# Joined small products, a split last tile and a new hand-written start in an attention-into-MLP kernel

## The chip, the core and the metric

The kernel runs on one core of one Trainium2 chip. The metric is the device time of one execution in microseconds (us), the median of several runs. The core has a matrix engine (TensorE, PE in the rows), VectorE (DVE), ScalarE (ACT), GpSimd (POOL) and a sync engine (SP) that issues most transfers. Each takes its own instructions strictly in order and waits at semaphores for the others. Matmul results go to PSUM banks of 128 rows by 512 fp32 columns; DVE and ACT carry them to SBUF.

## What is computed

```python
q_s = exp(q - max(q, -1)); q_s /= sum(q_s, -1) + 1e-9      # q, k, v: 8 x 8 x 576 x 64
k_s = exp(k - max(k, 2));  k_s /= sum(k_s, 2) + 1e-9       # k: softmax over the sequence
kv  = einsum('bhsd,bhde->...', k_s, v)                     # 64 x 64 per batch and head
x   = (q_s @ kv).transpose(0, 2, 1, 3).reshape(4608, 512)
h   = x @ w_in                                             # 512 x 2048
out = (h - tanh(h)) @ w_out                                # 2048 x 512
```

All is fp32. For the two large products, x, g = h − tanh(h) and both weights are split into a high and a low part, and three products (high·high, low·high, high·low) are added in PSUM.

## The kernel before

**Chunks and steps.** The 4608 tokens are worked on in 9 chunks of 512: one per batch, and one that collects the last 64 tokens of every batch. A chunk has 16 steps, one for each 128 columns of w_in. In a step TensorE makes `ph` (12 matmuls of 512 columns, `h_mm`), then ACT and DVE turn it into g by the chain u, t, vv, mk (ACT) and g, t, g, g (DVE); ACT casts the high part `gh`, and POOL or DVE subtracts it to get the low part `gl`. Two steps later (`LAG`) TensorE adds g times w_out into four banks `po`, one for 128 tokens each (`o_mm`, 12 matmuls). There are 144 steps. After a chunk's last step `o_out` copies the four `po` banks to SBUF and `o_store` writes them out.

**Small products.** Each batch also needs k^T v (`pk`, `kv_mm`) and q·kv (`px`, `x_mm2`). Both are fp32 matmuls: a `pk` has three parts, pk0 (first half of v, 16 instructions), then pk1 (second half, 16, and the last 64 rows, 8); a `px` has two halves px0 and px1 of 16 instructions each. They are spread over the steps of the chunk before. A bank from the pool `ps_m` holds each. The `px` halves are then cast to `xh` (ACT) and subtracted to `xl` (DVE), which the next chunk's `ph` reads. `v_ones` fills the tile of v for pk1 with columns of ones by POOL before its transfer.

**Order.** Up to step 33 the string `ORDER` names every operation one by one, in program order; a `*` picks the other engine (for `gl`, `sub`, `qu` and `qn` POOL without a star and DVE with one, for `cl` the reverse, for `ca` and `qs` ACT without). `phN` and `poN.t` are the large products of step N, `pk0@2` is batch 2's first `pk` part, `ld`, `cl`, `lo`, `pr`, `st`, `ca` and `sub` are the load and the splitting of one weight tile (`sub`, L213, makes its low part), `warm` are fp32 matmuls whose result nobody uses (`warm5h` is five; the trace counts an fp32 matmul as two), `out@b` and `in@b` send the maxima of k to memory and bring them back in a row shape (`rows<-most`, `row<-rows`), and `ks` subtracts them. From step 19 on the table `PLACES`, with `MOVED` for single batches, names for each of these the slot of a step (`first`, `ph`, `mid`, `sums`, `end`, `act`, `dve`, `dve2`, `pool`, `post`, `sp`) and the step counted from the chunk's start.

Of the kernel before, what the change touches and what calls it, by code (L numbers as in the profile page):

```python
# [37 lines left out]
sq3 px0 sub.i2 ld.i6 pr.i1 mq2 px2 xh0.1 xh0.0 ld.o5 warm10h st.i1 qu2 xh2.1 xl0.0 ca.i1 warm4h
sa3 ld.o3 xl0.1 xh2.0 lo.i3 sr3 xl2.0 qn6 qe2 xl2.1 ph0 ld.o2 km1.a vo1.2 lo.i5 sub.i1 sq2 lo.o0
v1.1 ca.i4 cl.i5 ph1 cl.o0 pr.i5 sa2 cl.i3 t0 km1.b ld.i7 u0 sr2 km1.c pr.i3 qn4 tt0 vv0 ph2 g0  # L40
pr.o0 st.i3 u1 t1 gg0 m0 km1.d vv1 cl.o1 pm1 ca.i3 st.o0 pt6 lo.o1 mx1 sub.i3 ph3 ca.o0 cp0 u2
mh1 g1 sub.i4 gh0 tt1 lo.i6 ml1 gg1 vo1.0 m1 qn7 v1.0 pb1 pr.o1 v1.2 cp1 ph4 t2 st.i5 cl.o2* m2
ld.o4 ks1.2 ld.i13 gh1 ld.o6 sub.o0* ca.i5 gl0 ld.o7 vv2 ks1.0 ld.o12 t3 u3 sub.i5 ph5 ks1.1
ld.i10 pr.o2 lo.o3 g2 gl1 ke1.0 qs6* ld.o8 pt4 gg2 ke1.1 qn5 po0.3 ld.i11 tt2 u4 po0.1 g3 qs4
cl.i6* po0.2 ld.o15 tt3 ke1.2 pt5 lo.o2 st.o1 cl.i7* pk1.0 cp2 qs5 ld.o9 vv3 st.o2 pk1.1 ca.o1
gg3 ld.i12 m3 sub.o1 pr.i6 cp3 pk1.2 t5 ld.o11 po0.0 st.i6 ca.o2 cl.o5 po1.1 lo.i7 cl.o3 cl.o4
gh2 po1.3 sub.o2* m4 gl2 po1.2 sl1 tt5 t4 pt7 pr.o3 rs1 rc1 po1.0 ca.i6* lo.o4 st.o3 po2.0 pr.o5
sub.i6 tt4 pr.i7 po2.1 g4 vv4 po2.2 st.i7 gh3 po2.3 u5 gg4 gl3 ph6 ca.i7 kn1 cp4 vv5 keep@1
pr.o4 sub.i7 g5 qs7* m5 st.o4 ca.o3 px4 lo.o5 cl.i12 gg5 ph7 lo.o6 sub.o3* ca.o4 ld.i9 cp5 xh4.1
ld.o10 sub.o4 u6 ld.o13 xl4.1 gh4 ld.o14 st.o5 k@2.2 xh4.0 po3.0 cl.o9 u7 po3.2 gl4* ld.i15  # L50
ca.o5 xl4.0 px6 t6 sub.o5 lo.o7 tt6 po3.3 cl.i10 xh6.0 ld.i14 cl.o6* po4.0 m6 xl6.0 po3.1 pr.i10
g6 cl.o15* po4.2 gh5 cl.o7* po4.3 xh6.1 gl5* vv6 po4.1 v@2.2 v@2.0 cl.i11* lo.i10 v@2.1 po5.0 g7
ld.i8 pr.o6 po5.1 gg6 cl.i9* xl6.1 po5.3 vv7 st.o6 ph8 t7 pr.i12 tt7 ca.o6 cp6 lo.i11 gg7 m7
cl.i15 pr.o7 po5.2 sub.o6* gh6 ph9 cl.o11 t8 st.o7 gl6 u8 cp7 vv8 tt8 lo.i12 g8 gh7 po6.0 st.i12
pr.i9 po6.2 gg8 m8 po6.1 ca.o7* lo.i8 gl7* po6.3 t9 sub.o7 lo.i15 ph10 tt9 cp8 u9 st.i10 gh8 g9
# [18 lines left out]
po20.0 exp0@2.0 gg22 ph25 cp22 u23 gl21* vv23 kf@2.0 t23 most@2.0 po20.1 po20.2 g23 out@2.0
po21.2 gh22 tt23 po21.1 t25 gl22* u25 po21.0 gg23 mu23 po21.3 cp23 in@2.0 po22.2 keep@0 sum0@2.0
gh23 po22.0 ph24 gl23* n01@2.0 tt25 g25 po23.0 n00@2.0 ks0@2.1 u24 po22.3 t24 po22.1 vv24 g24
mu24 ph26 gg24 tt24 vv25 gg25 cp24 po23.1 ks0@2.0 gh24 po23.2 t26 ph27 f01@2.0 mu25 ke0@2.0
gl24* cp25 out23.0 tt26 out23.1 u26 po23.3 g26 po24.1 gh25 ks1@2.0 pk0@2.0 vv26 t27 gg26 out23.2
ph28 gl25* mu26 v1@2.0 u27 f00@2.0 vv27 tt27 q1@2.0 g27 out23.3 po25.1 u28 cp26 po24.3 ke1@2.0
gg27 po24.2 mu27 po24.0 store23.2 vv28 v1@2.1 ph29 t28 v@2.3 ker@2.0 store23.1 gh26 gl26* cp27  # L80
po25.2 u29 g28 po25.0 max1@2.0 po25.3 po26.3 gh27 po26.2 mu28 gg28 sub1@2.0 t29 po26.0 tt28 vv29
po26.1 cp28 pk1@2.0 gl27* gh28 pk1@2.1 ph30 den@2.0 v@3.2 g29 v@3.0 den@2.1 den@2.2 tt29 gg29
gl28* po27.2 u30 den@2.3 po27.1 den@2.4 mu29 keep@2.0 po27.0 exp1@2.0 cp29 po28.2 g30 mu30
po27.3 sum1@2.0 vv30 k@3.0 po28.3 t30 k@3.2 gh29 px0@2.0 k@3.1 gl29 v@3.3 ph31 xh0@2.0 n11@2.0
xl0@2.0 gg30 n10@2.0 xh0@2.1 f11@2.0 po28.0 tt30 t31 back po28.1 f10@2.0 u31 cp30 po29.1 q0@3.0
# [954 lines left out]
```

## Time and profile before

| | |
|---|---|
| time, median of 3 runs | 882.75 us (882.49 to 883.05) |
| profiled execution | 882.5 us, its span 880.7 us |
| granted TensorE clock, mean | 0.998 |
| TensorE busy | 854.2 us, 97% of the span |
| VectorE busy | 668.8 us, 76% |
| ScalarE, GpSimd busy | 523.1 us (59%), 271.2 us (31%) |
| first matmul, last matmul's end | 14.40 us, 876.71 us |

The span runs from the first to the last instruction of the core; 1.8 us of the execution lie outside it. A row of a timeline gives the start, the duration, the engine, the line, the operation with its tiles, and in brackets the idle time ahead of it with the engine that ended it. Names are those of the program without their numbers.

### The profile page before, as it was taken

What the parts mean: (1) busy time and instruction counts of PE and PEld (TensorE: products, weight loads), DVE (VectorE), ACT (ScalarE), POOL (GpSimd) and SP (SyncE); (2) the same over time, 40 slices, a digit from 0 to 9 for tenths busy, and PEclk for the clock granted to TensorE, in tenths of its full rate; (3) what the DMA queues carried; (4) which work ended last, traced back from release to release, by engine and by line L of the source; (5) the groups of instructions that cost most, each with busy time, mean ns of one, the idle gap of its engine ahead of it and who ended that gap; (6) DMA issues with size and microseconds to landing.
All of it is one profiled execution on the core that took longest, in us unless ns stands there. A gap on an engine that the chain in (4) does not pass through costs nothing.

```text
span 880.7 us, 13278 instructions
## 1 busy us (share of the span) xinstructions
PE 854.2 (97%) x4860; PEld 699.7 (79%) x4860; DVE 668.8 (76%) x1102; ACT 523.1 (59%) x914; POOL 271.2 (31%) x233
## 2 busy tenths in 40 slices
PE   3999999989999999999999999999999999999998
PEld 2877888768788888888888888888888888888886
DVE  7898999978887879678867787768866776655444
ACT  4887987546455556555665565555555555555553
POOL 3664222111233323332234233323323333322221
PEclk9999999999999999999999999999999999999999
DMA  9996130004523315331432232322261011002001
GB/s 258 329 316 208 45 76 1 0 19 109 131 85 49 90 25 60 49 91 24 60 49 61 54 52 50 68 55 19 43 96 32 1 48 25 1 1 49 1 0 48
DMA packets 127873, 61.17 MB, mean 69 GB/s; under 512 B 72768, under 2 KB 118848, under 8 KB 127808
## 3 DMA queue, kind: packets, MB, share of 16 engines
q1 hardware_dynamic: 127808, 60.32, 30.5%
q8 instruction: 38, 0.62, 0.3%
q14 instruction: 27, 0.22, 0.1%
HBM read 48.76 MB, written 11.55 MB: 68 GB/s over the span
## 4 chain that ended last, share of the span: by engine, by line
PE 82%; DVE 10%; DMA 3%; ACT 2%; issue 2%; SPq 0%; DVEq 0%; ACTq 0%
PE po L853 39%; PE ph L775 38%; DVE g L809 2%; PE pk L364 2%; DMA rows<-most 2%; PE px L631 2%; DVE g L804 1%; DVE g L796 1%; PE warm L233 1%; DMA row<-rows 1%; DMA k<-in_k_dram 1%; DVE t L801 1%; DVE k L350 1%; PE px L596 1%; DVE gl L815 0%
## 5 line engine op out<-in xcount | busy, mean ns | idle before, releaser
L853 PE MATMUL po<-w_o,gh 128*128 128x512 f32 x1152 | 356.5, 391 | 1.5 <-ACT o L885 1.0
L775 PE MATMUL ph<-xh,w_i 128*128 128x512 f32 x1152 | 312.0, 393 | 1.8 <-DVE t L801 1.7
L815 POOL TENSOR_TENSOR gl<-g,gh 128x512 fp32r<-128x512 f32 x121 | 161.5, 1335 | 462.3 <-ACT gh L812 452.9
L775 PEld LDWEIGHTS ph<-xh,w_i 128*128 128x128 f32 x1152 | 214.6, 188 | 49.6 <-DVE t L801 2.1
L853 PEld LDWEIGHTS po<-w_o,gh 128*128 128x128 f32 x1152 | 215.1, 188 | 48.2 <-ACT o L885 1.4
L853 PE MATMUL po<-w_o,gl 128*128 128x512 f32 x576 | 224.5, 390 | 0.2 <-POOL gl L815 0.2
L796 DVE SCALAR_TENSOR_TENSOR g<-u,ph 128x512 f32<-128x512 f32 x144 | 98.2, 682 | 161.4 <-ACT t L790 157.7
L812 ACT CAST gh<-g 128x512 fp32r<-128x512 f32 x144 | 89.7, 623 | 212.6 <-DVE g L809 196.1
L775 PE MATMUL ph<-xl,w_i 128*128 128x512 f32 x576 | 154.7, 390 | 0.0
L790 ACT ACTIVATE u<-ph 128x512 f32<-128x512 f32 x144 | 86.3, 599 | 98.4 <-PE ph L775 97.6
L775 PEld LDWEIGHTS ph<-xl,w_i 128*128 128x128 f32 x576 | 108.5, 188 | 23.1
L853 PEld LDWEIGHTS po<-w_o,gl 128*128 128x128 f32 x576 | 108.1, 188 | 23.6 <-POOL gl L815 0.6
L809 DVE COPY_PREDICATED g<-mk,t 128x512 f32<-128x512 int32 x144 | 116.0, 805 | 13.7 <-ACT mk L790 1.8
L790 ACT ACTIVATE vv<-u,b_pa 128x512 f32<-128x512 f32 x144 | 104.7, 727 | 8.4 <-DVE g L804 8.3
L804 DVE SCALAR_TENSOR_TENSOR g<-vv,g 128x512 f32<-128x512 f32 x144 | 106.8, 742 | 0.9 <-ACT vv L790 0.6
L801 DVE TENSOR_TENSOR t<-ph,t 128x512 f32<-128x512 f32 x144 | 98.3, 683 | 1.9 <-ACT t L790 1.7
L790 ACT ACTIVATE t<-ph 128x512 f32<-128x512 f32 x144 | 85.5, 594 | 4.7 <-PE ph L775 4.2
L790 ACT ACTIVATE mk<-u 128x512 int32<-128x512 f32 x125 | 78.8, 630 | 2.4 <-DVE g L809 2.4
L522 POOL TENSOR_TENSOR q<-q,sq 128x512 f32<-128x512 f32 x28 | 32.8, 1175 | 34.2 <-DVE sq L502 34.2
L522 POOL TENSOR_TENSOR q<-q,mq 128x1024 f32<-128x1024 f32 x14 | 27.9, 1992 | 30.5 <-DVE mq L526 18.5
L663 DVE TENSOR_TENSOR xl<-px,xh 128x512 fp32r<-128x512 f32 x36 | 23.6, 690 | 2.5 <-ACT xh L661 2.5
L661 ACT CAST xh<-px 128x512 fp32r<-128x512 f32 x36 | 19.6, 587 | 3.6 <-PE px L596 2.3
(105 smaller groups left out, 580.1 us busy)
## 6 DMA issues: line engine op xcount, KB each, us to landing
k<-in_k_dram SPq DMA_DIRECT2D x16, 512.0 KB, 5.6
raw_i<-in_moe_w_in_dram SPq DMA_DIRECT2D x16, 512.0 KB, 7.6
raw_o<-in_moe_w_out_dram SPq DMA_DIRECT2D x16, 512.0 KB, 8.4
v<-in_v_dram SPq DMA_DIRECT2D x14, 512.0 KB, 4.4
out_dram<-o SPq DMA_DIRECT2D x28, 256.0 KB, 6.4
q<-in_q_dram SPq DMA_DIRECT2D x48, 128.0 KB, 4.0
q<-in_q_dram SPq DMA_DIRECT2D x3, 512.0 KB, 7.2
row<-rows SPq DMA_DIRECT2D x6, 256.0 KB, 4.5
```

The source lines that it names most:

```text
L522: nc.gpsimd.tensor_tensor(part, part, of, op=op)
L661: nc.scalar.copy(xh, px)
L663: nc.vector.tensor_tensor(xl, px, xh.bitcast(F32), op=ALU.subtract)
L775: nc.tensor.matmul(ph, w[:, i, c], x[:, c, :], start=(n == 0), stop=(n == len(ops) - 1))
L790: nc.scalar.activation(new(tag, **of), st[src], fn, **kw)
L796: nc.vector.scalar_tensor_tensor(new("g"), st["u"], C2, st["ph"], op0=ALU.mult, op1=ALU.mult)
L801: nc.vector.tensor_tensor(st["t"], st["ph"], st["t"], op=ALU.subtract)
L804: nc.vector.scalar_tensor_tensor(st["g"], st["vv"], PB, st["g"], op0=ALU.add, op1=ALU.mult)
L809: nc.vector.copy_predicated(st["g"], st["mk"], st["t"])
L812: nc.scalar.copy(new("gh", F32R), st["g"])
L815: eng.tensor_tensor(new("gl", F32R), st["g"], st["gh"].bitcast(F32), op=ALU.subtract)
L853: nc.tensor.matmul(po[t], g[:, cols], wt["o", f][:, w], start=(begin and n == 0), stop=(end and n == 2),)
```

## The change

- **Joined runs.** pk0 moves from the middle of step 5 to the end of step 7, in front of pk1; px0 moves from the end of step 9 to the end of step 12, in front of px1. For this the second v tile (`v1`) gets a place of its own, the batch's still empty `xl` buffer, and is filled from step 1 on; px1 takes two banks of the pool `ps_h` (that of `ph`). The first `pk` pair so joined is batch 2's, the first `px` pair batch 3's; there are six of each. In a step with a joined `px` the next step's `po` is also put behind it, before the next `ph`. The transfer of v1 now stands ahead of the transfers `out@b` or `in@b` on SP.
- **Last tile.** The last chunk's last `po` tile is made in two banks: 384 columns in its own and 128 in a bank `more`. ACT copies the bank in two pieces, DVE adds `more`, and two transfers write it.
- **New start.** The string for the first 34 steps is another one. In numbers of operations by engine:

| operation | before | after |
|---|---|---|
| warm instructions | 34 | 25 |
| `gl` on POOL, on DVE | 12, 22 | 5, 29 |
| `sub` on POOL, on DVE | 20, 15 | 11, 24 |
| `cl` on DVE, on POOL | 21, 11 | 19, 13 |
| `qu` on POOL, on DVE | 3, 1 | 2, 2 |
| `qs` on DVE, on ACT | 3, 5 | 2, 6 |

- **Batch 4.** Its exponentials `ke0` and `ke1` stand one step later (steps 5 and 6), behind the subtractions `ks0` and `ks1`, now both in step 4; `kf` and `most` are in slot `dve2`.

```diff
 ORDER = """
-q0 q1 k0.0 vo0.1 k0.1 vo0.0 vo1.1 k0.2 ld.i0 ld.i2 q3 mq0 ld.i4 qu0* v0.0 mq1 qe0 km0.a v0.1 qu1
+q0 q1 k0.0 vo0.0 k0.1 vo0.1 k0.2 ld.i0 ld.i2 q3 mq0 ld.i4 qu0* v0.0 mq1 qe0 km0.a v0.1 qu1 sq0
...
+    def x_place(j: int) -> int:
+        n = ROUND.index(j)
+        return n if n < 2 else (n + 1) % 2
...
+            elif u and b >= HALVED:
+                at = B if b == B - 1 else b
+                vt = xp.tile([P, H, 2 * D + 2], F32, name=f"v{b}_{u}", tag=f"xl{x_place(at)}")
...
+    JOINED = 3
...
-        px_of[i] = px = [q_psum(i, f"px{i}_{j}") for j in range(2)]
+        if u and ROUND.index(b) >= JOINED:
+            px = [ps_h.tile([P, NC, P], F32, name=f"px{i}_{j}", tag="h") for j in range(2)]
+        else:
+            px = [q_psum(i, f"px{i}_{j}") for j in range(2)]
...
-        pk0=("mid", 5), v1=("pool", 5), pk1=("end", 7), den=("dve", 8), keep=("sp", 9),
+        pk0=("end", 7), v1=("pool", 1), pk1=("end", 7), den=("dve", 8), keep=("sp", 9),
...
-        px0=("end", 9), xh0=("late", 9), xl0=("dve", 10),
+        px0=("end", 12), xh0=("post", 12), xl0=("post", 12),
...
-        px1=("end", 12), xh1=("late", 12), xl1=("dve", 13),
+        px1=("end", 12), xh1=("late", 12), xl1=("dve", 12),
...
+        4: dict(kf=("dve2", 1), most=("dve2", 1), out=("sp", 1), **{"in": ("sp", 2)}, ks0=("dve", 4), ke0=("act", 5), ke1=("act", 6)),
...
+        parts = [(po[turn], slice(0, DM), begin)]
+        if last:
+            parts = [(po[turn], slice(0, DM - P), begin), (spare["more"], slice(DM - P, DM), True)]
+        for bank, at, first in parts:
...
+            if (j, t) == (ROUND[-1], TPC - 1):
+                nc.scalar.copy(o[:, : DM - P], po[:, : DM - P])
+                nc.scalar.copy(o[:, DM - P :], po[:, DM - P :])
+                at = slice(DM - P, DM)
+                nc.vector.tensor_tensor(o[:, at], spare["more"][:, at], o[:, at], op=ALU.add)
...
+            if n - 1 in joined:
+                put(n - 1, "end", f"po{n - LAG}.{t}")
```

On TensorE, in a chunk of the second half, `pk` stood in two places 30 rows apart before (`ph_5` to `ph_8` are the large products of four successive steps):

```order
950 L775 MATMUL ph_5_4470<-xh_3884,w_i_615 128x512 x4
951 L364 MATMUL pk_4483<-v_0_3953,k_0_3947 64x65 x16
952 L853 MATMUL po_0_0_4348<-w_o_874,gh_3_4417 128x512 x2
...
981 L853 MATMUL po_0_3_4360<-w_o_912,gl_5_4530 128x512
982 L364 MATMUL pk_4483<-v_1_4532,k_1_3949 64x65 x16
983 L364 MATMUL pk_4483<-vr_3956,kr_3951 64x65 x8
984 L775 MATMUL ph_8_4658<-xh_3884,w_i_1358 128x512 x4
```

In the same chunk after, the three parts stand in one place, ahead of `ph_8`:

```order
986 L879 MATMUL po_0_3_4374<-w_o_978,gl_5_4527 128x512
987 L376 MATMUL pk_4614<-v_0_3940,k_0_3934 64x65 x16
988 L376 MATMUL pk_4614<-v_1_4332,k_1_3936 64x65 x16
989 L376 MATMUL pk_4614<-vr_3943,kr_3938 64x65 x8
990 L792 MATMUL ph_8_4669<-xh_4085,w_i_1367 128x512 x4
```

The number of `pk` instructions is the same, and one border between them and the large products is gone.

On VectorE, around the row exchange of batch 2 (`most` goes to memory, `row` comes back, the first row that reads `row` is the subtraction from k), before:

```order
248 L336 TENSOR_TENSOR most_1882<-most_1882,more_1884 32x16
249 L796 SCALAR_TENSOR_TENSOR g_15_1895<-u_15_1872,ph_15_1827 128x512
...
259 L801 TENSOR_TENSOR t_9_1907<-ph_9_1858,t_9_1907 128x512
260 L796 SCALAR_TENSOR_TENSOR g_9_1961<-u_9_1911,ph_9_1858 128x512
261 L350 TENSOR_TENSOR kr_934<-kr_934,row_1923 64x512
262 L796 SCALAR_TENSOR_TENSOR g_8_1980<-u_8_1968,ph_8_1944 128x512
```

And after:

```order
259 L348 TENSOR_TENSOR most_1882<-most_1882,more_1884 32x16
260 L832 TENSOR_TENSOR gl_13_1904<-g_13_1799,gh_13_1902 128x512
...
277 L818 TENSOR_TENSOR t_8_2011<-ph_8_1946,t_8_2011 128x512
278 L826 COPY_PREDICATED g_8_1979<-mk_8_2016,t_8_2011 128x512
279 L362 TENSOR_TENSOR k_0_1321<-k_0_1321,row_1968 128x1024
280 L832 TENSOR_TENSOR gl_8_2046<-g_8_1979,gh_8_2029 128x512
```

Between the last row of `most` and the first use of `row` stood 12 rows (a row of four small copies counted once), and now stand 19.

## Rows read from the trace of the kernel before

**Rows 1.** The page's part 1 (busy us, share, instructions) and part 4.

```profile
PE 854.2 (97%) x4860; PEld 699.7 (79%) x4860; DVE 668.8 (76%) x1102; ACT 523.1 (59%) x914; POOL 271.2 (31%) x233
PE 82%; DVE 10%; DMA 3%; ACT 2%; issue 2%; SPq 0%; DVEq 0%; ACTq 0%
```

**Rows 2.** TensorE's waits: waiting line, releaser, us in total, times, longest.

```profile
PE ph L775 <- DVE t L801: 1.7, 1, 1.7
PE px L596 <- DVE spare_qs L581: 1.7, 1, 1.7
...
PE ph L775 <- ACT w_i L209: 0.2, 1, 0.2
```

**Rows 3.** TensorE's timeline, 429 to 482 us: three stretches with small products.

```profile
442.85 1.07 PE L775 MATMUL ph<-xh,w_i 128*128 128x512 f32 x4
...
449.61 1.07 PE L775 MATMUL ph<-xh,w_i 128*128 128x512 f32 x4
...
457.77 0.62 PE L853 MATMUL po<-w_o,gh 128*128 128x512 f32 x2
...
465.15 0.62 PE L853 MATMUL po<-w_o,gh 128*128 128x512 f32 x2
...
470.59 0.62 PE L853 MATMUL po<-w_o,gh 128*128 128x512 f32 x2
...
477.33 0.62 PE L853 MATMUL po<-w_o,gh 128*128 128x512 f32 x2
```

**Rows 4.** TensorE's timeline, 22 to 34 us: the first chunk's small products.

```profile
22.46 1.15 PE L364 MATMUL pk<-v,k 128*64 128x65 f32 x32
...
25.09 3.62 PE L233 MATMUL warm<-ident 128*128 128x128 f32 x30
28.63 1.10 PE L596 MATMUL px<-spare_qs,kvs 64*64 64x128 f32 x32
...
30.54 3.39 PE L233 MATMUL warm<-ident 128*128 128x128 f32 x28
33.69 1.18 PE L775 MATMUL ph<-xh,w_i 128*128 128x512 f32 x4
```

**Rows 5.** DVE's timeline: the row that frees the first `px`.

```profile
25.81 0.42 DVE L385 TENSOR_TENSOR kvs<-pk,rs 128x256 f32<-128x256 f32 x1
```

**Rows 6.** DVE, groups of instructions by shape, 33 to 160 us (count, busy us, mean ns).

```profile
L809 DVE COPY_PREDICATED g<-mk,t 128x512 f32<-128x512 int32 x20 | 20.4, 1021 | 2.0 <-ACT mk L790 1.8
L804 DVE SCALAR_TENSOR_TENSOR g<-vv,g 128x512 f32<-128x512 f32 x20 | 16.5, 824 | 0.6 <-ACT vv L790 0.4
L801 DVE TENSOR_TENSOR t<-ph,t 128x512 f32<-128x512 f32 x21 | 14.4, 685 | 1.5 <-ACT t L790 1.4
```

**Rows 7.** The same view of DVE, 420 to 613 us (a stretch with whole weights).

```profile
L809 DVE COPY_PREDICATED g<-mk,t 128x512 f32<-128x512 int32 x33 | 24.9, 755 | 3.4
L804 DVE SCALAR_TENSOR_TENSOR g<-vv,g 128x512 f32<-128x512 f32 x33 | 24.0, 727 | 0.0
```

**Rows 8.** The same view of POOL, 33 to 160 us.

```profile
L815 POOL TENSOR_TENSOR gl<-g,gh 128x512 fp32r<-128x512 f32 x10 | 16.6, 1656 | 36.1 <-ACT gh L812 26.8 <-DVE raw_o L191 8.3 <-POOL w_i L213 1.0
```

**Rows 9.** DVE's timeline: two successive operations in the start.

```profile
55.68 0.67 DVE L796 SCALAR_TENSOR_TENSOR g<-u,ph 128x512 f32<-128x512 f32 x1
56.27 0.68 DVE L801 TENSOR_TENSOR t<-ph,t 128x512 f32<-128x512 f32 x1
```

**Rows 10.** DVE's timeline: the row exchange of batch 2.

```profile
187.27 0.68 DVE L350 TENSOR_TENSOR kr<-kr,row 64x512 f32<-64x512 f32 x1 [4.13 <-DMA row<-rows]
```

**Rows 11.** TensorE's timeline: a wait near step 19.

```profile
159.65 0.73 PE L853 MATMUL po<-w_o,gh 128*128 128x512 f32 x2 [0.55 <-ACT gh L812]
```

**Rows 12.** Busy time and granted clock (the tenths after POOL), 74 to 76 us.

```profile
74.00:76.00 2.00, 2.00 (x6) 1.60 (x5) 2.00 (x4) 2.00 (x5) 1.63 (x1) 0.53 1.09 409
```

**Rows 13.** TensorE's and DVE's timelines: the end.

```profile
876.32 0.39 PE L853 MATMUL po<-w_o,gl 128*128 128x512 f32 x1
876.75 0.69 DVE L883 COPY o<-po 128x512 f32<-128x512 f32 x1 [0.60 <-PE po L853]
```

More of the change, by code (lines that the diff above doesn't have):

```diff
@@ L38 @@
[L38 to L55, printed above, removed]
@@ L74 @@
[L74 to L85, printed above, removed]
@@ new lines @@
+sa0 km0.b qe1 km0.c sr0 km0.d sq1 cl.i0* pm0 qn1 pr.i0 warm1h mx0 lo.i0 warm1h vo0.2 lo.i2
+v0.2 mh0 ml0 pb0 sa1 sr1 cl.i2 ld.i1 qn2 mq3 pt1 ks0.0 lo.i4 cl.i4* warm1h qs1 warm1h qn0 ks0.2
+ke0.0 warm1h ks0.1 warm1h qn3 q2 warm1h pr.i2 warm1h ld.o0 st.i0 pr.i4 warm1h ld.i3 pk0.0
+ke0.1 st.i2 qu3* warm1h ca.i2 warm1h k1.0 pk0.1 ke0.2 sub.i2* qe3 st.i4 pk0.2 ca.i0 k1.1 warm1h
+cl.i1 warm1h sl0 ld.i5 lo.i1 pt0 sub.i0 rs0 rc0 k1.2 sq3 pt2 qs0 warm1h warm1h ld.i6 pr.i1 pt3
+kn0 ld.o1 warm1h qs2 st.i1 warm1h px0 qs3 cl.o0* ld.o3 sa3 mq2 ca.i1 warm1h vo1.0 px2 xh0.0
@@ new lines @@
+po20.0 vv23 kf@2.0 po20.2 t23 cp22 exp0@2.0 po20.3 most@2.0 ph25 gh21 gl21* out@2.0 tt23 g23
+po21.3 t25 gg23 po21.0 gh22 po21.2 mu23 gl22* po21.1 cp23 po22.3 sum0@2.0 gh23 ph24 u25 gl23*
+n01@2.0 tt25 po22.0 in@2.0 u24 n00@2.0 v1@2.1 po23.0 vv24 g24 keep@0 po23.3 g25 po22.2 gg24 ph26
+f00@2.0 vv25 out23.3 t24 out23.0 tt24 mu24 cp24 po22.1 v@2.1 ks0@2.0 t26 po23.1 gh24 ph27 u26
+gl24* ke0@2.0 tt26 ks1@2.0 mu25 po23.2 g26 u27 gg25 po24.3 out23.2 po24.1 cp25 ke1@2.0 ph28
+ks0@2.1 vv26 f01@2.0 mu26 q1@2.0 t27 tt27 pk0@2.0 out23.1 u28 ker@2.0 pk1@2.0 gh25 k@3.0 pk1@2.1
@@ L91 @@
+px1@2.0 km0@3.0 gh30 po29.1 g31 xh1@2.0 gl30 back po29.3 xh1@2.1 xl1@2.0 mu31 keep@2.0 po29.2
+tt31 po29.0 xl1@2.1 gg31 ph32 cp31 km1@3.0 km2@3.0 po30.1 km3@3.0 u32 ph33 g32 vv32 gh31 t32
+gl31 mu32 tt32 po30.3 gg32 u33 po30.0 cp32 t33 po31.0 vv33 g33 mu33 po30.2 tt33 po31.3 gg33 gh32
+out31.0 po31.2 gl32* po31.1 out31.3 cp33 store31.3 out31.2 gh33 out31.1 max0@3.0 store31.1
+keep@1 gl33* sub0@3.0 v@3.3 store31.2 v@3.0 v@3.1 store31.0
 """
@@ L848, in o_mm @@
         end = f == NF - 1 or (j == 0 and f == F0 - 1)
+        turn = j, j == 0 and f >= F0, t
         if begin:
-            po[t] = ps_o.tile([P, DM], F32, name=f"po{j}_{f}_{t}", tag="o")
+            po[turn] = ps_o.tile([P, DM], F32, name=f"po{j}_{f}_{t}", tag="o")
         cols = slice(t * P, (t + 1) * P)
-        for n, (g, w) in enumerate(((gh, 0), (gh, 1), (gl, 0))):
-            nc.tensor.matmul(
-                po[t],
-                g[:, cols],
-                wt["o", f][:, w],
-                start=(begin and n == 0),
-                stop=(end and n == 2),
-            )
+        last = (j, f, t) == (ROUND[-1], NF - 1, TPC - 1)
+        if last:
+            spare["more"] = ps_m.tile([P, DM], F32, name="more", tag="m")
+        parts = [(po[turn], slice(0, DM), begin)]
+        if last:
+            parts = [(po[turn], slice(0, DM - P), begin), (spare["more"], slice(DM - P, DM), True)]
+        for bank, at, first in parts:
+            for n, (g, w) in enumerate(((gh, 0), (gh, 1), (gl, 0))):
+                nc.tensor.matmul(
+                    bank[:, at],
+                    g[:, cols],
+                    wt["o", f][:, w, at],
+                    start=(first and n == 0),
+                    stop=(end and n == 2),
+                )
         if end:
-            spare["po", j, f, t] = po[t]
+            spare["po", j, f, t] = po[turn]
     def o_aside(t: int):
@@ L965, in attn_moe_kernel @@
     put(2 * NF, "post", "back")
+    joined = {NF * (n - 1) + (PLACES | MOVED.get(n, {}))["px1"][1] for n in range(JOINED, NCH)}
     for n in range(PLANNED, len(steps)):
         for t in range(TPC):
-            put(n, "first" if n == 2 * NF else "sums", f"po{n - LAG}.{t}")
+            if n - 1 in joined:
+                put(n - 1, "end", f"po{n - LAG}.{t}")
+            else:
+                put(n, "first" if n == 2 * NF else "sums", f"po{n - LAG}.{t}")
             if steps[n - LAG][1] == NF - 1:
```

88 lines of the change are left out of this document (52 added, 36 removed).

## The prediction

> **What bounds the kernel now.** I read first the busy shares and the chain that ended last [rows 1]. TensorE works 854.2 of 880.7 us, and the chain runs 82% over it and 10% over VectorE. Of the 26.5 us without work, 14.4 lie ahead of the first matmul and 4 (880.7 − 876.71) behind the last; the other 8.1 are waits inside. So little can come from fewer waits, and the rest only from matmuls that are paid twice or run slowly.
>
> Second, TensorE's list of waits [rows 2]: behind the first matmul it has eleven entries between 1.7 and 0.2 us, 8.2 us together. All lie before 227 us, as TensorE's timeline shows. From there on TensorE never waits, and a change there counts only by what TensorE itself has to do. Before that VectorE releases most of the waits, so there the balance between VectorE and GpSimd counts too. About 4.6 us of the waits lie before 160 us and 3.6 between 188 and 226 us.
>
> Third, the timeline of TensorE where no wait is left [rows 3]. A step's pair of `ph` and `po` takes 470.59 − 465.15 = 5.44 us. Where a small product stands between, the same distance, between neighbouring `ph` or `po`, is longer: 449.61 − 442.85 = 6.76 around pk0, 465.15 − 457.77 = 7.38 around pk1 with its rest, and 477.33 − 470.59 = 6.74 around one `px`. So pk0 costs 1.32 us, pk1 with the rest 1.94, one `px` half 1.30: 5.86 a batch.
>
> **The joined runs.** In the first chunk the same products stand back to back [rows 4]. The three parts of `pk` take 25.09 − 22.46 = 2.63 us, against 1.32 + 1.94 = 3.26 spread out; two `px` halves take 30.54 − 28.63 = 1.91, against 2.60. Part of that is no border but what comes behind: there the run ends in small matmuls, here in a `ph`, and the `ph` behind a small product is itself longer. So I take about half of the differences 0.63 and 0.69, 0.24 to 0.37 a pair with 0.29 between. Six `pk` and six `px` make 12 × 0.29 = 3.5 us (2.9 to 4.4). They fall on TensorE where it bounds the time, so all of it counts.
>
> What it could wait for: px1 now holds two banks of `ph`, until its `xh` and `xl` have left them. With a batch's px0 and px1 in one place (I took the steps around 491 us and put the new order on them) px1 would end about 493.1, the `po` put behind it keeps TensorE until 495.9, and the four `xl` end at 494.4 to 495.0 with ACT and VectorE as busy as they are now. So `ph` has 0.9 to 1.5 us in hand, an estimate; if that were missed it would be missed six times. The transfer of v1 stands ahead of the row exchange on SP. It is put out only after GpSimd's fill of ones, which is behind a `gl`; but `pk0` comes two steps later than before, so a late `row` reaches TensorE only through VectorE standing at `ks0`. I take nothing, at most 1 us over all batches.
>
> **The start, up to the first step.** Before, 30 warm matmuls (3.62 us) keep the first `px` until 28.63, though its input kvs is ready at 25.81 + 0.42 = 26.23 [rows 4, 5]; 28 more keep `ph` until 33.69. After, six warm instructions of 0.24 us (3.62 / 15) and three transposes of q of some 0.5 stand between the end of the first `pk` and the first `px`, about 3 us, and six more, 1.45 us, between the second `px` half and `ph`. VectorE gets a subtraction of 128x1024, a reduction and a weight's low part ahead of kvs and loses two smaller ones, some 1.4 us more, so kvs comes about 27.6. `px` then begins about 27.7, takes 1.9 us and one warm (0.24), and with 1.45 us of warms behind it `ph` of step 0 begins about 31.3 instead of 33.69: 2.4 us earlier. That is worth something only where TensorE is not held up afterwards.
>
> **Steps 0 to 19.** Sixteen low parts (gl 7, sub 9) go from GpSimd to VectorE. One costs VectorE 0.60 us, the distance of two starts [rows 9]: +9.6 us. The other trades (two `cl` and a `qs` away from VectorE, a `qu` to it) come to −0.7, an estimate. Net +8.9 us, and VectorE has only some 8 us of idle time from 33 to 160 us.
>
> Against that stands what GpSimd's work costs VectorE. In this stretch the predicated copy takes 1021 ns and the sum g<-vv,g 824, while the later stretch, with less of GpSimd, has 755 and 727 [rows 6, 7]. The t<-ph,t, which reads PSUM, takes 685 as ever. So 20 × (266 + 97) ns = 7.3 us are lost to something that only the operations with SBUF inputs feel. GpSimd's element-wise work in the stretch is about 50 us; six `gl` at 1.66 us [rows 8] and about six weight parts at 1.5 go, 38% to 41% of it. In proportion 2.8 to 3.0 us come back, up to 3.7 with the stretched weight operations.
>
> The Trainium skill bears on this: "GPSIMD Engine Reference", section "8. Key points", says that GpSimd shares its SBUF interfaces with VectorE and names contention with VectorE instructions that have two SBUF inputs or run in a 2-port mode; it also calls VectorE about twice as fast on element-wise work. The trace agrees in both: the operation with a PSUM input is not stretched, and a low part takes 1656 ns there against 0.60 us here. By this rule the move gives 3 us back; without it the sum below would be 3.7 us higher, which is what the slower rival assumes.
>
> At step 19 (`po` at 159.65 waits 0.55 us for `gh`, [rows 11]) the shift is then +8.9 − 3.7 − 5 for half of the idle time that a fuller VectorE can use, together nothing, from −4.6 (TensorE alone bounds, all its waits of this stretch go) to +5.2 (no idle time is used). A longer 2.0 us of half clock follows the wait at 71.95: 74 to 76 us have 0.53 [rows 12], the lower of two levels, 1.2 GHz. With the wait it would go, about 1 us; I leave it inside the bounds.
>
> **Steps 19 to 33.** Here VectorE stands 4.13 us for `row` at 187.27 [rows 10], and behind it in its queue are the g and t of two steps; TensorE then waits 1.66 for a t and 0.99 for an `o` copy. Now 19 rows stand between `most` and its use, 12.1 us of work by their rows' durations against 7.3 before. The exchange took 187.27 − 175.68 = 11.6 us, so the wait goes. Three of the low parts that moved lie here as well, and TensorE's 3.6 us of waits do not all go: −3.0 (−3.6 to 0). For the whole new order then −3.0, bounds −8.2 and +5.2.
>
> **The end.** The last matmul starts at 876.32 and the copy of its tile at 876.75, 0.69 long [rows 13]; the store follows. With three matmuls of 128 columns last, at some 0.12 each by the warm ones (3.62 / 30), the first 384 columns are done about 0.15 to 0.3 sooner and ACT's copy of them (0.6) lies beside. Then comes an addition of 128 columns, some 0.3, in place of 0.69, but behind ACT's second copy. One store of a quarter ends sooner than a whole one, but a second one is to be issued. −0.4, from −0.8 to +0.3.
>
> **Batch 4.** ACT's two exponentials go one step back. TensorE waits for nothing in those steps, so 0; if `pk0` were late by it, it has two steps in hand.
>
> **Sum.** On the profiled execution (882.5, 0.25 under the median): −3.5 − 3.0 − 0.4 = −6.9, or 875.6, and 875.8 against the median.
>
> **The rivals.**
>
> *VectorE does not bind the start.* All waits after step 0 go and the earlier first step is kept: −4.6 − 3.6 − 3.5 − 0.4 = −12.1, or 870.6. For it speaks that no wait but four is over 1 us and that GpSimd's slow low parts are behind several of them; against it VectorE's 92% between 40 and 160 us.
>
> *The joins give nothing.* Either the border costs the same wherever it stands, or `ph` waits for its banks as much as a border is worth: 882.75 − 3.4 = 879.3. For it speaks that [rows 4] show joined runs only between other small matmuls.
>
> *Slower.* The low parts make VectorE the bound in steps 2 to 19 with no time given back and no idle time to take: +8.9 at step 19, where `po` waits for `gh` already. It decides from a shift of 6.9 on, where it eats all the rest: +8.9 − 6.9 = +2.0, or 884.7. For it speaks the busy share of VectorE there, and that the idle waits are for ACT, which is not moved; against it the stretched copies.
>
> *The clock.* With 25 instead of 34 warm instructions, and gaps in between, the lower level could be granted when `ph` begins. Each 2 us of `ph` at half clock lose about 1 us, as from 74 to 76 us [rows 12]; three such stretches with a start without gain and the joins kept are 882.75 − 3.9 + 3 = 881.9.
>
> **How the numbers follow.** Forecast 0.54, no VectorE bound 0.20, joins nothing 0.12, slower 0.11, clock 0.03. A measurement of this kernel tells 0.2%, 1.8 us, from no change, so "same" is 881.0 to 884.5. The slower case lies on that line, 0.08 beyond and 0.03 inside; the clock's 0.03, 0.01 of the forecast and 0.01 of the joins are inside too: faster 0.84, same 0.08, slower 0.08. The likeliest case's own range is 872 to 880; with most of the first two rivals it is 869.5 to 882.
>
> **What would show it.** Joins: the distance of `po` around a joined `px` pair should be 5.44 + 2.3 us or less and around a joined `pk` 5.44 + 3.0, with no wait at the `ph` behind. Start: `ph` of step 0 about 31.3, and step 19's `po` near where it is now, within 5 us. Contention: the predicated copy's mean from 33 to 160 us below 0.95 us. Row exchange: no idle VectorE at the first `ks0`. End: less than 4.0 us from the last matmul's end to the span's end. I am wrong if step 19 comes later than 165 us, if waits of over 0.3 us appear on `ph` at the six joined steps, or if VectorE now waits for GpSimd's v1.

## The result and the profile after

The changed kernel takes 867.72 us (867.2 to 867.92), the kernel before on the same chip 882.62: a ratio of 0.9829 (0.9812 to 0.9847), 14.9 us less. The forecast was 875.8, its range 869.5 to 882.0. The profiled execution has a span of 865.8 us against 880.7.

The page's part 1 and part 4 of the changed kernel answer to [rows 1]:

```profile
PE 845.4 (98%) x4845; PEld 699.0 (81%) x4845; DVE 662.9 (77%) x1115; ACT 520.7 (60%) x917; POOL 246.4 (28%) x219
PE 91%; ACT 3%; DMA 2%; SPq 1%; DVE 1%; issue 1%; POOL 0%; ACTq 0%
```

TensorE works 8.8 us less and is idle 6.1 us less. VectorE has left the chain (10% to 1%). Where TensorE's idle time went is in its list of waits, to be read beside [rows 2]:

```profile
PE pm L304 <- DVE km L298: 13.3, 1, 13.3
PE px L607 <- ACT spare_qs L593: 1.2, 1, 1.2
PE px L607 <- DVE xl L679: 0.7, 1, 0.7
PE ph L792 <- DVE xl L679: 0.7, 1, 0.7
PE ph L792 <- ACT w_i L217: 0.4, 1, 0.4
PE pb L325 <- DVE mh L313: 0.2, 1, 0.2
```

Behind the first matmul, 3.2 us of waits stand against 8.2, and the first matmul comes 1.1 earlier. No wait is left behind 76 us. The four at 159.65, 190.00, 194.71 and 226 are gone. VectorE reaches batch 2's subtraction behind a short wait for ACT's mk, and does not wait for `row` any more:

```profile
181.58 0.76 DVE L826 COPY_PREDICATED g<-mk,t 128x512 f32<-128x512 int32 x1 [0.32 <-ACT mk L807]
182.23 1.21 DVE L362 TENSOR_TENSOR k<-k,row 128x1024 f32<-128x1024 f32 x1
```

[rows 10] had 4.13 us at this place. The timeline of TensorE at a joined `pk` and a joined `px` answers to [rows 3]:

```profile
444.33 0.62 PE L879 MATMUL po<-w_o,gh 128*128 128x512 f32 x2
...
447.14 2.08 PE L376 MATMUL pk<-v,k 128*64 128x65 f32 x64
449.16 0.68 PE L376 MATMUL pk<-vr,kr 64*64 64x65 f32 x16
449.77 0.50 PE L792 MATMUL ph<-xh,w_i 128*128 128x512 f32 x1
...
452.63 0.62 PE L879 MATMUL po<-w_o,gh 128*128 128x512 f32 x2
...
474.39 0.62 PE L879 MATMUL po<-w_o,gh 128*128 128x512 f32 x2
...
477.20 1.98 PE L649 MATMUL px<-qs,kvs 64*64 64x128 f32 x64
479.11 0.74 PE L879 MATMUL po<-w_o,gh 128*128 128x512 f32 x2
...
482.00 1.07 PE L792 MATMUL ph<-xh,w_i 128*128 128x512 f32 x4
```

From 474.39 to 482.00 lie two `po` groups (5.44) and the `px` pair: 7.61 − 5.44 = 2.17 us, against 2.60 apart, 0.43 less. The next `po` behind the joined `pk` and its `ph` starts at 452.63, so the `pk` costs 452.63 − 444.33 − 5.44 = 2.86 against 3.26, 0.40 less. The `ph` behind has no idle time in brackets: the banks that px1 borrows are free in time.

The start of the small products answers to [rows 4], VectorE's groups between 33 and 160 us to [rows 6], and the last rows to [rows 13]:

```profile
27.13 1.10 PE L607 MATMUL px<-spare_qs,kvs 64*64 64x128 f32 x32
...
29.62 1.80 PE L241 MATMUL warm<-ident 128*128 128x128 f32 x12
31.47 1.20 PE L792 MATMUL ph<-xh,w_i 128*128 128x512 f32 x4
33.34 1.33 PE L792 MATMUL ph<-xl,w_i 128*128 128x512 f32 x4 [0.68 <-DVE xl L679]
...
861.59 0.27 PE L879 MATMUL more<-w_o,gl 128*128 128x128 f32 x1
862.29 0.29 DVE L912 TENSOR_TENSOR o<-more,o 128x128 f32<-128x128 f32 x1 [1.12 <-ACT o L910]
```

```profile
L826 DVE COPY_PREDICATED g<-mk,t 128x512 f32<-128x512 int32 x21 | 16.4, 781 | 0.2
L821 DVE SCALAR_TENSOR_TENSOR g<-vv,g 128x512 f32<-128x512 f32 x22 | 15.8, 716 | 0.3
L818 DVE TENSOR_TENSOR t<-ph,t 128x512 f32<-128x512 f32 x22 | 15.0, 684 | 0.7 <-ACT u L807 0.5 <-ACT t L807 0.2
```

The first `ph` is at 31.47 (31.3 was forecast). The predicated copy is down from 1021 to 781 ns and the sum from 824 to 716, close to the 755 and 727 of [rows 7]; t<-ph,t stays.

**How a VectorE operation loses time beside GpSimd.** From 33 to 160 us GpSimd's busy time falls from 49.2 to 29.2 us, by 41%, as the prediction had it; but of the 7.3 us that these two operations lost there, nearly all came back. So it was not a matter of proportion. Two pairs of rows of the kernel before show what happens. First GpSimd's instruction, then VectorE's that began behind it:

```profile
8.63 1.90 POOL L488 TENSOR_TENSOR spare_q<-spare_q,mq 128x1024 f32<-128x1024 f32 x1 [6.89 <-DVE mq L483]
8.66 2.42 DVE L280 TENSOR_TENSOR km<-k 128x512 f32<-128x512 f32 x1
...
155.99 2.30 POOL L522 TENSOR_TENSOR q<-q,mq 128x1024 f32<-128x1024 f32 x1 [2.75 <-DVE mq L526]
156.42 2.47 DVE L809 COPY_PREDICATED g<-mk,t 128x512 f32<-128x512 int32 x1
```

GpSimd ends at 10.53 and VectorE at 11.08; GpSimd at 158.29 and VectorE at 158.89. VectorE ends 0.55 to 0.60 behind GpSimd, about what it takes alone (0.7): it stood until GpSimd's instruction was done. In the first 230 us I took every single VectorE instruction that is over 0.12 us longer than the shortest of its form. There are 24 before, 17.4 us longer in sum, and 10 after, 5.1 us, each beside a GpSimd instruction. That is 12.3 us back (1.75 of it is the first row above, told of next). Between 33 and 160 us, the stretch of the forecast, 11.4 us went down to 2.6: 8.9 back, where 2.8 to 3.7 were forecast.

The first pair also explains the first matmul, which waits for km. (This first maximum of two k tiles is what the expectations below call the first copy of k.) In the profile after, VectorE is first and takes 0.69, and GpSimd takes 2.34 in place of 1.90:

```profile
8.61 0.69 DVE L292 TENSOR_TENSOR km<-k 128x512 f32<-128x512 f32 x1
8.72 2.34 POOL L500 TENSOR_TENSOR spare_q<-spare_q,mq 128x1024 f32<-128x1024 f32 x1 [6.98 <-DVE mq L495]
```

The order of these two is the same in both kernels; 0.1 us decides. The 1.1 us are so not due to the change: executions of the old order (e1, e3) have the first matmul at 13.4 and 13.1 too. Nor need they last: in e1 the first `ph` begins at 33.70, in the kernel before at 33.69 (in e3 at 32.68).

### The profile page after: what moved, and what is told of

It reads as the page before. It is cut to its first block, busy times and chain, and to the rows that moved or that the text cites. A ratio compares the mean times of both kernels' runs of the same rounds, so it can differ in the third digit from the quotient of the medians.

```text
span 865.8 us, 13247 instructions
## 1 busy us (share of the span) xinstructions
PE 845.4 (98%) x4845; PEld 699.0 (81%) x4845; DVE 662.9 (77%) x1115; ACT 520.7 (60%) x917; POOL 246.4 (28%) x219
## 4 chain that ended last, share of the span: by engine, by line
PE 91%; ACT 3%; DMA 2%; SPq 1%; DVE 1%; issue 1%; POOL 0%; ACTq 0%
PE po L879 45%; PE ph L792 43%; DMA raw_i<-in_moe_w_in_dram 2%; PE pk L376 2%; PE px L649 2%; ACT raw_o L203 0%; SPq L247 0%; ACT raw_o L206 0%; DVE xl L679 0%; ACT t L807 0%; ACT gh L829 0%; ACT w_o L217 0%; SPq L480 0%; PE px L607 0%; ACT vv L807 0%
## 5 line engine op out<-in xcount | busy, mean ns | idle before, releaser
L792 PE MATMUL ph<-xh,w_i 128*128 128x512 f32 x1152 | 307.3, 390 | 0.4 <-ACT w_i L217 0.4
L832 POOL TENSOR_TENSOR gl<-g,gh 128x512 fp32r<-128x512 f32 x114 | 149.1, 1308 | 429.7 <-ACT gh L829 386.7
L826 DVE COPY_PREDICATED g<-mk,t 128x512 f32<-128x512 int32 x144 | 109.7, 762 | 12.6 <-DVE g L821 0.5
L821 DVE SCALAR_TENSOR_TENSOR g<-vv,g 128x512 f32<-128x512 f32 x144 | 104.2, 724 | 0.5
L807 ACT ACTIVATE t<-ph 128x512 f32<-128x512 f32 x144 | 85.3, 593 | 11.4 <-PE ph L792 10.1
L832 DVE TENSOR_TENSOR gl<-g,gh 128x512 fp32r<-128x512 f32 x30 | 20.7, 691 | 3.7 <-ACT gh L829 3.5
```

The costliest lines, as they stand in the source:

```text
L792: nc.tensor.matmul(ph, w[:, i, c], x[:, c, :], start=(n == 0), stop=(n == len(ops) - 1))
L807: nc.scalar.activation(new(tag, **of), st[src], fn, **kw)
L821: nc.vector.scalar_tensor_tensor(st["g"], st["vv"], PB, st["g"], op0=ALU.add, op1=ALU.mult)
L826: nc.vector.copy_predicated(st["g"], st["mk"], st["t"])
L832: eng.tensor_tensor(new("gl", F32R), st["g"], st["gh"].bitcast(F32), op=ALU.subtract)
```

## The experiments

Each kernel is timed beside the kernel before on its chip. The runs are from three further chips, on which the kernel before takes 879.99 to 880.82 us. The changed kernel itself was run on two of them: on that of e5 to e8 (e5: 867.68, 867.27 to 867.88) and, later than e1 to e4, on theirs (e15: 866.97, 866.24 to 867.75). On that of e9 to e12 it was not run. Where no other run is named, a difference is against 867.7; for e1 to e4 it would be 0.7 us more against e15. Of the edits only the lines that matter are shown, and of the string's lines the piece around the edit.

**e5 and e15: the changed kernel again.**

> The changed kernel as it is, as the measure for the runs beside it on this chip: 0.983 of the kernel before. If the kernel before's first copy of k meets GpSimd's subtraction on this chip too, the gap is 15 us, if not 13 to 14.

> The changed kernel as it is, as the measure for the two runs beside it: 867.7.

Ratios of 0.9858 (0.9842 to 0.9875) and 0.9845 (0.983 to 0.9859): 12.3 and 13.4 us; the first is less than either case expected. The changed kernel is as fast as on the first chip, the kernel before some 2 us faster. Why stays open, as there is no trace of the kernel before from these chips. The first step of km does not show it: its 1.0 us are gone by the first `ph` of e1. Nor does the mean granted clock of the kernel before, 0.997 to 1.0 there and 0.998 in the first chip's profile.

**e1: the old start.** The string of the first 34 steps as before, all else as changed.

```diff
 ORDER = """
-q0 q1 k0.0 vo0.0 k0.1 vo0.1
+q0 q1 k0.0 vo0.1 k0.1 vo0.0
...
```

> The changed kernel with the old order of the first 34 steps; joined runs, last tile and batch 4 as changed. Theory: the new start is worth 9.8 us (1.1 from the earlier first matmul, 5.0 from waits of TensorE, 2.2 from nine warm instructions fewer, 1.3 from the stretch at half clock), so 877.5 us (876.5 to 878.5), with TensorE's waits behind the first matmul back at 7 to 9 us. Rival: the joins and the last tile carry most of the gain (10 us); then 870 to 872.

875.97 us (875.52 to 876.35), 8.3 more than the changed kernel and under the 876.5 to 878.5 expected. TensorE's waits behind the first matmul are back at 7.1 us (8.2 before, 3.2 after). So the start is worth 8.3, and its parts are not those named there: the first matmul is at 13.40 here too, and e7 and e8 below take the warm instructions out of the sum. The half clock of [rows 12] is no part either: behind the same wait of 1.65 us the granted clock is 1.00 from 72 to 76 us here, where the kernel before had 0.62 and 0.53.

**e2: the old engines.** The new order, with the 24 low parts whose engine differs (20 moved to VectorE, 4 away) back on the old one.

```diff
-sub.i2*
+sub.i2
...
-gl0*
+gl0
...
-sub.o1*
+sub.o1
...
```

> The changed kernel in its own order, but each low part (gl, sub) of the first 34 steps on the engine that it had before. Theory: a VectorE operation with SBUF inputs that starts while GpSimd computes stands until GpSimd's instruction ends, so what the move gives back is these stretches (17.4 us before, 5.1 after in the first 230 us): they rise to over 10 us, TensorE's waits from 3.2 to 5 to 7, time 870 to 872. Rival: the new sequence alone avoids the meetings; stretches stay under 8 us and the time at 867.5 to 868.5. Rival from the prediction: VectorE's own load binds, so 16 low parts less on it make it faster, under 867.

872.67 us (871.71 to 873.45), 5.0 more and a little over the 872 expected, with 16 operations less on VectorE. The stretches are 17.9 us: 12.8 more, against 9.6 of work less (16 × 0.60). Rows of VectorE and of GpSimd in it:

```profile
67.59 1.51 POOL L832 TENSOR_TENSOR gl<-g,gh 128x512 fp32r<-128x512 f32 x1 [0.33 <-POOL v L270]
67.88 1.77 DVE L821 SCALAR_TENSOR_TENSOR g<-vv,g 128x512 f32<-128x512 f32 x1
69.34 1.45 POOL L221 TENSOR_TENSOR w_i<-c_i,w_i 128x512 fp32r<-128x512 f32 x1 [0.25 <-ACT w_i L217]
69.68 1.70 DVE L826 COPY_PREDICATED g<-mk,t 128x512 f32<-128x512 int32 x1
```

Both times VectorE ends 0.55 to 0.59 behind GpSimd. The sequence alone does not avoid the meetings. That TensorE waits for GpSimd's slower low parts does not explain it: GpSimd releases one wait of 0.2 us here.

**e3: the new engines in the old order.** The same 24 on the new engine, in the kernel before.

```diff
-sub.i2
+sub.i2*
...
-gl0
+gl0*
...
```

> The kernel before in its own order, but each low part of the first 34 steps on the engine that the changed kernel gives it. Theory: the stretches of VectorE fall from 17.4 to 9 to 11 us and nearly pay for the 8.9 us added; waits fall a little, 879 to 882 us. Rival (the prediction's load): VectorE gets fuller and step 19 comes up to 5 us later, 885 to 888. Rival (sequence does it): no change, 882.3 to 883.

877.31 us (876.71 to 877.54) against 880.82, a ratio of 0.9962 (0.9947 to 0.9977): 3.5 us faster, though VectorE has 16 operations more; 879 to 882 was expected. Its stretches fall from 17.4 to 7.9 us (1.75 of that is the first step of km). The load of the prediction (885 to 888) does not come. But 7.8 us back for 9.6 of work would leave VectorE 1.8 fuller, so this sum does not give the 3.5 us, and what does stays open.

**e12: all low parts on VectorE.** The 13 that GpSimd still had in the 34 steps as well.

```diff
-sub.i0
+sub.i0*
...
-gl1
+gl1*
...
```

> The changed kernel with the 13 low parts of the first 34 steps that GpSimd still makes on VectorE too (5 gl, 8 sub). Theory (VectorE's time counts, its own work and its stretches alike): 13 x 0.60 = 7.8 us more work against at most 3 of the remaining 5.1 us of stretches, so VectorE is up to 5 us fuller and the time 1 to 4 us longer, 869 to 872. Rival (what counted was GpSimd's slowness in making a low part that TensorE waits for): no change or up to 1 us faster, 866.7 to 867.8.

875.97 us (875.71 to 878.35), 8.3 more, twice the 4 us expected at most. The stretches rise from 5.1 to 8.5 us in place of falling (the rest of GpSimd's work meets others), so VectorE gets 7.8 us of work and 3.4 of stretches more. TensorE waits 1.86 us for a t, and the granted clock behind it is 0.56 and 0.59 for 4 us:

```profile
49.82 0.49 PE L182 MATMUL warm<-ident 128*128 128x128 f32 x2 [1.86 <-DVE t L759]
...
50.00:52.00 2.00, 2.00 (x9) 1.72 (x10) 2.00 (x5) 1.20 (x3) 0.28 (x1) 0.56 1.11 301
```

The second row is of the view of windows, and 0.56 is the granted clock. So VectorE is the bound in the start, and the rival of e12 is out. That a stall weighs as much as work fits e2 and e12 in sign; their sizes (3.2 us more on VectorE for 5.0, and 11.2 for 8.3) do not show it one for one.

**e7 and e8: warm instructions.** Nine more ahead of the first step, and none at all.

```diff
-xl2.0 warm1h ld.o2 qn6 qe2 xl2.1 ph0
+xl2.0 warm1h ld.o2 qn6 qe2 warm9h xl2.1 ph0
...
```

> The changed kernel with nine more warm instructions ahead of the first step (34 in all). Theory: after the first step TensorE is hardly held up, so what stands ahead of it counts in full except the 0.7 us it waits there for xl: +1.5 us. Rival (VectorE binds the start, the first step's time does not matter): no change.

> The changed kernel without any of its 25 warm instructions. Theory: TensorE waits for the other engines where most of them stood, so at most 1 us is gained there; if the clock then falls to its lower level in the first steps, each 2 us of it cost 1 us and the time is 1 to 3 us longer. Rival (warm instructions are pure cost): 25 x 0.24 = 6 us less.

867.54 us (867.31 to 867.9) with nine more, 868.32 (866.68 to 868.55) with none, against e5's 867.68: no change within the spread. e7 is a miss of the theory. In e8 neither the gain nor the loss came, and the granted clock is 1.00 from 14 to 42 us. When the first `ph` begins does not matter. Why, two pairs of rows show, of the changed kernel and then of e7: the first step of km on VectorE, and the first `px` of batch 1 on TensorE.

```profile
33.81 1.32 DVE L292 TENSOR_TENSOR km<-k 128x512 f32<-128x512 f32 x1
...
63.92 0.43 PE L607 MATMUL px<-spare_qs,kvs 64*64 64x128 f32 x2
```

```profile
33.09 1.18 PE L792 MATMUL ph<-xh,w_i 128*128 128x512 f32 x4
...
34.17 1.33 DVE L292 TENSOR_TENSOR km<-k 128x512 f32<-128x512 f32 x1
...
64.27 0.43 PE L607 MATMUL px<-spare_qs,kvs 64*64 64x128 f32 x2
```

From the end of km to that `px` are 63.92 − 35.13 = 28.79 and 64.27 − 35.50 = 28.77 us. In all twelve profiles with this order and these engines up to there it is 28.68 to 28.82, while the first `ph` lies between 30.85 and 33.09. In the changed kernel's first profile VectorE has 0.2 us of idle time from 31 to 73 us. And what shifts this `px` shifts the end one for one: it lies between 63.11 and 64.41 in the three profiles of the changed kernel, in e7 and in e8, and the execution's time less its start is 803.6 to 803.8 us in all five.

**e13: only the late low parts back.** The 17 of the 24 that stand behind the ninth step's `ph` in the order.

```diff
 ph8
...
-gl6*
+gl6
...
-sub.o10*
+sub.o10
...
```

> The changed kernel with the old engine for the 17 low parts of the first 34 steps that stand behind the ninth step's ph in the order; the seven ahead of it keep the new engine. Theory (VectorE's time counts in the first 75 us or so, where it has no idle time, and little later): of the 5.0 us that all 24 cost when put back, 3.8 came by 84 us, so 1.1 us here, 868.6 to 869.0. Rival (the low parts cost the same wherever they stand): 17/24 of 5.0, 871.2.

868.25 us (867.58 to 868.84), 1.3 more than e15 beside it, with ranges that overlap. From that `px` to the `pk` of batch 2 it takes 127.68 us against 127.01; the other 0.6 lie ahead of the `px`, where runs differ by as much without an edit. So the late moves are worth 0.7 to 1.3 us, and the seven early ones carry three quarters or more of the 5.0.

**e14: one stall taken away.** A clamp moved behind the four `xl`, and the old last tile.

```diff
-xh0.1 ld.o4 cl.i3
+xh0.1 ld.o4
...
-xl2.1 ph0
+xl2.1 cl.i3 ph0
...
```

> The changed kernel with the old last tile (0.3 us) and one operation of VectorE, the clamp of one weight tile, moved from ahead of the first chunk's four xl to behind them. There it waited 0.82 us for its transfer and then stood 1.15 us for GpSimd's subtraction of 128x1024. Theory: VectorE bounds from 31 to 73 us, so what it gets back counts one for one: 1.2 to 2.0 us, 865.4 to 866.2. Rival (the first steps' time is set by TensorE or ACT, as 9 warm instructions more cost nothing): only the tail, 867.2 to 867.6.

866.78 us (866.25 to 866.87), 0.2 less than e15: no gain that can be told, a miss. The clamp met the next GpSimd instruction instead:

```profile
32.24 1.30 POOL L221 TENSOR_TENSOR w_i<-c_i,w_i 128x512 fp32r<-128x512 f32 x1
32.60 1.23 DVE L199 TENSOR_SCALAR raw_i<-raw_i 128x512 f32<-128x512 f32 x1
```

VectorE was through with km at 34.43 instead of 35.13, 0.7 us of the 2.0, and the `px` came 0.7 earlier (63.22), one for one. In e15 the clamp started later beside GpSimd and was through early by itself (34.31, `px` 63.11). In the changed kernel itself km ends at 34.31 to 35.20 (e15, e5), so the first steps differ by 0.9 us from run to run, and this edit is inside it.

**e9: a dose of GpSimd.** One more subtraction by GpSimd in each step of chunks 4 (512 columns) and 5 (256).

```diff
+            if j in (4, 5):
+                n = CH if j == 4 else CH // 2
+                u = st["u"][:, :n]
+                nc.gpsimd.tensor_tensor(u, u, u, op=ALU.subtract)
             nc.vector.copy_predicated(st["g"], st["mk"], st["t"])
```

> The changed kernel with one more GpSimd subtraction in each step of chunks 4 and 5 (about 375 to 560 us), on u after its last use, of 128x512 in chunk 4 and 128x256 in chunk 5; it is let go when ACT's mk ends, just before VectorE's g<-vv,g. Theory (VectorE's operation stands until GpSimd's instruction ends): in chunk 4 that g lasts about 1.3 us longer than GpSimd's instruction minus their difference of starts, so its mean goes from 0.72 to 1.5 to 1.8 us, in chunk 5 to 1.0 to 1.2. Rival (the two engines share, so that each loses in proportion): in both chunks the same small stretch while they overlap, 0.9 to 1.1 us in chunk 4 and 0.8 to 0.95 in chunk 5. t<-ph,t, which reads PSUM, unchanged by both. Time: TensorE bounds, 867.7 to 868.5.

Rows with 512 and with 256 columns:

```profile
409.68 0.68 DVE L818 TENSOR_TENSOR t<-ph,t 128x512 f32<-128x512 f32 x1
410.18 1.04 POOL L829 TENSOR_TENSOR u<-u 128x512 f32<-128x512 f32 x1 [0.81 <-ACT mk L807]
410.28 1.48 DVE L821 SCALAR_TENSOR_TENSOR g<-vv,g 128x512 f32<-128x512 f32 x1
...
534.69 0.62 POOL L829 TENSOR_TENSOR u<-u 128x256 f32<-128x256 f32 x1 [0.66 <-ACT mk L807]
534.79 1.06 DVE L821 SCALAR_TENSOR_TENSOR g<-vv,g 128x512 f32<-128x512 f32 x1
```

In another step VectorE is first:

```profile
479.89 0.68 DVE L821 SCALAR_TENSOR_TENSOR g<-vv,g 128x512 f32<-128x512 f32 x1
479.92 1.56 POOL L829 TENSOR_TENSOR u<-u 128x512 f32<-128x512 f32 x1 [0.88 <-ACT mk L807]
480.68 1.41 DVE L830 COPY_PREDICATED g<-mk,t 128x512 f32<-128x512 int32 x1
```

In the first two pairs GpSimd ends at 411.22 and 535.31, VectorE at 411.76 and 535.85: 0.54 behind, both times. GpSimd's instruction is 0.42 us shorter, and so is VectorE's. That is standing until the end, not sharing. It is so in 20 of the 32 steps. In the other 12 GpSimd's instruction is the one that gets longer (1.44 to 1.83 in place of 1.04, 1.02 to 1.40 in place of 0.62), and the predicated copy, which begins behind it, stands (up to 1.42 us). In 10 of these VectorE's g begins first; in two it begins 0.25 us behind GpSimd by the trace, which the theory does not explain. By these 12 the means missed the theory: 1.21 us in chunk 4 and 0.92 in chunk 5, the second within the rival's range, so the single rows decide here.

The size of e9's cost was a miss too: 873.99 us (873.85 to 874.76), 6.3 more, where at most 0.8 was expected. TensorE waits 4.6 us more, at chunk borders for `o` copies and once for a t. VectorE's stretches between 380 and 575 us are 21.7 us in place of 6.5; it seems that this exhausts its slack even in the later chunks.

**e4 and e10: the joins undone.** `px` and `pk` apart again (e10 with batch 4's old places, which it needs).

```diff
-        px0=("end", 12), xh0=("post", 12), xl0=("post", 12),
+        px0=("end", 9), xh0=("late", 9), xl0=("dve", 10),
...
```

```diff
-        pk0=("end", 7), v1=("pool", 1), pk1=("end", 7), den=("dve", 8), keep=("sp", 9),
+        pk0=("mid", 5), v1=("pool", 1), pk1=("end", 7), den=("dve", 8), keep=("sp", 9),
...
```

> The changed kernel with px0 and px1 of batches 3 to 8 in their old two places and in the old banks; everything else as changed. Theory: each joined px pair saves 0.43 us of border, six of them 2.6: 870.3 us (869.9 to 870.7). Rival (half of the difference, as predicted): 0.29 each, 869.5. Rival (joined px costs a wait elsewhere): no change, 867.7.

> The changed kernel with pk0 of batches 3 to 7 back in the middle of step 5, pk1 where it is, and batch 4's exponentials back (they have to be there in time for pk0). Theory: a joined pk saves 0.40 us of border, five of them 2.0: 869.7 us (869.3 to 870.1), plus what batch 4 costs (nothing). Rival (0.29 each, as predicted): 869.1.

e4: 870.54 us (869.8 to 870.85), 2.8 more for six `px` pairs. e10: 870.22 (869.61 to 870.64), 2.0 more than e11 beside it, for five `pk`. That is 0.47 and 0.40 a pair, near the 0.43 and 0.40 of the timeline after, and not 0.29. In e4's profile, from batch 1's first `px` to the end, it is 2.5 us for six, 0.42 each.

**e6: the old last tile.**

```diff
-        last = (j, f, t) == (ROUND[-1], NF - 1, TPC - 1)
+        last = False
...
```

> The changed kernel with the last tile in one bank, one copy by VectorE and one store, as before. Prediction: the split is worth 0.4 us, so this is 0.4 slower than the changed kernel. Theory from the trace after: the split makes the last matmuls 0.13 longer and VectorE's addition waits 1.12 us for ACT's second copy, so it is worth nothing: within 0.2 us of the changed kernel.

867.35 us (867.3 to 867.49), 0.3 less than e5 beside it, whose range it overlaps. The split gains nothing and may cost 0.3.

**e11: batch 4 at the common places.**

```diff
-        4: dict(kf=("dve2", 1), most=("dve2", 1), out=("sp", 1), **{"in": ("sp", 2)}, ks0=("dve", 4), ke0=("act", 5), ke1=("act", 6)),
```

> The changed kernel with batch 4's kf, most, ks0, ke0 and ke1 at the common places. Theory and prediction: TensorE waits for nothing there, so no change, 867.5 to 867.9. Rival: the row exchange with v1's transfer ahead of it comes late at the common places and VectorE stands at ks0; then TensorE waits 0.5 to 1.5 us once, 868.2 to 869.

868.20 us (867.57 to 869.14). One wait appears, at the border of batch 3's chunk to batch 4's, that the changed kernel has not:

```profile
327.14 0.73 PE L878 MATMUL po<-w_o,gh 128*128 128x512 f32 x2 [0.50 <-DVE o L913]
```

So the edit is worth about 0.5 us, by this wait and the median; the ranges overlap. The releaser is VectorE's copy of an `o`, which points to VectorE's order at the border and not to the exponentials' lateness.

## Why the prediction was wrong

- **Steps 0 to 19: the term that failed.** The prediction gave VectorE "2.8 to 3.0 us ... up to 3.7" back for +8.9 us of moved work, by proportion to GpSimd's busy time. The runs give 8.9 us back in the same stretch, 33 to 160 us, and 12.3 in the first 230 us (9.5 with the engines alone, e3). That step failed: the stretched operation does not lose a share, it stands until GpSimd's instruction ends (e9). So without the first step of km VectorE got 10.6 back for 8.9 and is not 5 us fuller but 1.7 emptier, and a shift of the first `px`, at 64 us, passes on to the end one for one. The prediction had the shift at step 19 as "together nothing"; the engines alone were worth 5.0 us (e2). The Trainium skill ("GPSIMD Engine Reference", section "8. Key points") names the right operations, as the row of t<-ph,t shows; that section gives no size, and the proportion was my reading.
- **The first step at 31.3** was right to 0.2 us and of no value. That it "is worth something only where TensorE is not held up afterwards" was the right reserve: e7 shifts it by 1.6 us for nothing.
- **Steps 19 to 33** came as forecast or better: the wait for `row` went, and all of the 3.6 us of TensorE's waits. The other waits were read a little wrong: 4.3 us lie before 160, not 4.6, and one of 0.2 is at 265, behind the 227 us named.
- **The joins** were right in mechanism. I took half of the differences 0.63 and 0.69; 0.40 and 0.43 came, so 6 × 0.83 = 5.0 us in place of 3.5. The mis-sized term is the border behind the run: the `ph` or `po` there loses some 0.2 us, not half of the saving. The worry about px1's banks did not come true.
- **The end:** −0.4 forecast, about 0 to +0.3 measured. VectorE's addition waits 1.12 us for ACT's second copy of the bank, and the six shorter matmuls end 0.13 later than three long ones.
- **Batch 4:** 0 forecast, some 0.5 gained (e11).
- **The sum.** −6.9 was forecast and −14.9 came: −3.0 against −8.3 for the start (e1), −3.5 against −5.0 for the joins. With 0.5 for batch 4 and up to 0.3 lost at the end that is some 13.5, where e5 and e15 have 12.3 and 13.4; the 1.5 us or more on the first chip stay open (see e5). The rival "VectorE does not bind the start" came nearest with 870.6, but by a wrong reason: VectorE does bind there (e12, and the constant 28.8 us). The slower rival asked the right question, what VectorE's load does, and left the stalls out.

It stays open where the other 3.3 us (e1 less e2) of the new start come from: the moves of its sequence were not tried one by one. No version tried beats the changed kernel by more than the spread (e14, e6).

## What to carry to other kernels

Where VectorE has no idle time, count its instructions and its stalls: look for VectorE instructions longer than the shortest of their form, and whether they end half a microsecond behind a GpSimd instruction. Each such meeting costs the rest of GpSimd's instruction, so GpSimd work moved to VectorE can be worth more than the VectorE time that it takes (e2, e3), though moving all of it cost 8.3 us (e12). To set it beside VectorE's reads of PSUM, which keep their 0.68 us in e9, was not tried. A join of small matmul runs was worth here about two thirds of the difference between together and apart.
